# Decode attention with a gated MLP mixer: value products placed behind the second half of the scores, first keys loaded head by head, four tiny loads ahead of the output weights

## The chip, the cores and the metric

The kernel runs on one NeuronCore of a Trainium2 chip. The metric is the device time of one execution in microseconds (us), lower is better. A time "of the runs" is the median of several executions; a "span" is the stretch of one profiled execution that the profile covers, which is a little shorter than that execution's own time.

Five engines work side by side, each through its own list of instructions in order: TensorE (PE in the profile; its weight loads are PEld), VectorE (DVE), ScalarE (ACT), GpSimd (POOL) and SyncE (SP), which here issues the loads. Engines wait for one another through semaphores.

## The reference

One decode step for 8 batch rows. Attention over the last 1024 cached positions, with 16 query heads on 8 key/value heads of width 256, is mixed with an MLP of width 1792 through a sigmoid gate. Everything is bf16 with D = 448.

```python
W = min(4096, max(256, Sk // 4))                  # 1024 of 4096 positions
q = (x @ wq).reshape(B, Sq, Hq, Dh)               # Hq 16, Dh 256
scores = einsum("bhqd,bhkd->bhqk", q, k) * Dh ** -0.5
p = softmax(scores)
a = einsum("bhqk,bhkd->bhqd", p, v) ... @ wo
b = gelu(layernorm(x) @ w1 + b1) @ w2 + b2
g = sigmoid((x * gate_w).sum(-1))
out = g * a + (1 - g) * b
```

Keys and values of the window are 8 x 8 x 1024 x 256 x 2 bytes = 33.6 MB each; with the weights some 77.7 MB are read once.

## The kernel before, in words

**Units.** The cache is worked through in 16 units `u`: one batch row and 4 of the 8 key/value heads (`QUAD`). The keys of a unit are one tile of 128 partitions x 8192 bf16 (2 MB): partition 4s + a holds positions of head a, 32 consecutive ones (`kv_loader`, L109). The values of a unit have the same form.

**Loads.** All large loads go through `plan`, a list in a fixed order: keys 0, query weights, the MLP's weights, then keys u followed by values u-2 (`LAG` is 2), at the end values 14 and 15 and the output weights `wo` (L155 to L176). They share a ring of 9 slots of 2 MB. `pump` (L99) issues the next load on SyncE's queue as soon as `done` has been told that a slot's reader is recorded; in the built program a load's issue waits for that reader, and also for the landing of the load eight places ahead of it in the list, because eight completion semaphores take turns. The slot of the keys is released by the second `turn_keys` of the unit, that of the values by `values`.

**One turn of the loop** (L613 to L630) carries four units at different stages. The steps, by name:

- `turn_keys(u, hf)`, L356: VectorE turns half of the keys into `kt` (32x32 transposes).
- `scores(u, hf)`, L422 and L428: TensorE writes half of the scores into PSUM tile `S`: one product that masks foreign heads (L422) and eight with the keys (L428).
- `top(u-1)`, L440 and L442: VectorE takes the maximum `mx` of the previous unit's scores and spreads it into `m4`. `share(u-1)`, L448: a small fp32 product `mz` joins the maxima.
- `expo(u-1)`, L454 and L457: VectorE reduces `mz` to `nmx`; ScalarE computes `E = exp(S + nmx)` and its row sums.
- `turn(u-2)`, L470: VectorE transposes `E` into `ET`. `total(u-2)`, L481: TensorE adds up the row sums (`den`, fp32). `invert(u-2)`, L491 and L492: VectorE's reciprocal `rb`, ScalarE's `rsel`.
- `values(u-2)`, L500 and L509: sixteen TensorE products `PO <- slot, ET`, then ScalarE's copy `first` of one half of `PO`.
- `gather(u-3)`, L515: VectorE adds the other half of `PO` to `first`, giving `os_`. `finish(u-3)`, L530 and L533: fp32 products `fin`, copied by ScalarE into `oT`.

The order is written out by hand: the pool context is `manual_schedule`, so each engine executes its own steps in the order in which the Python calls them. In the loop `values(u-2)` stands between the two halves of `scores(u)` on TensorE, and `first(u-2)` and `rsel(u-2)` stand ahead of `E(u-1)` on ScalarE. `PO` is a single PSUM tile, the score tiles `S` are two, and the fp32 products `den`, `mz` and `fin` share two small tiles.

**After the loop** (L631 to L686) the last units run out: `turn`, `total`, `top(15)`, `share(15)`, `gather(13)`, `finish(13)`, `invert(14)`, `expo(15)`, `values(14)`, `turn(15)`, `total(15)`, `invert(15)`, `gather(14)`, `finish(14)`, then `spread_rows` (L655), `values(15)`, `gather(15)`, `finish(15)`, `spread_rows`, and `project` (L671): 128 small products with the output weights into `A_ps`, the mix `res` (L688) and four stores.

Of the kernel before, what the change touches and what calls it, by code (L numbers as in the profile page):

```python
# [11 lines left out]
BF16 = mybir.dt.bfloat16  # L12
# [6 lines left out]
def kernel(  # L19
# [15 lines left out]
    nc = tc.nc  # L35
    P = nc.NUM_PARTITIONS

    NB, Sq, D = A_x.shape
    _, Hkv, Sk, Dh = A_k_cache.shape
# [19 lines left out]
    QUAD = 4  # L59
    RQ = QUAD * rep  # L60
    NQ = NB * Hkv // QUAD
    SK = P // QUAD
    NCK = W // SK
# [9 lines left out]
    LAG = 2  # L73
# [7 lines left out]
    xf = A_x.rearrange("b s d -> (b s) d")  # L81
# [3 lines left out]
    consts = ctx.enter_context(tc.tile_pool(name="consts", bufs=1))  # L85
# [19 lines left out]
    def done(n=1):  # L105
        consumed[0] += n
        pump()

    def kv_loader(src, u, parts):  # L109
        b, half = divmod(u, Hkv // QUAD)  # L110
        v = src[b, half * QUAD : (half + 1) * QUAD, kv_base:Sk, :].rearrange(
            "a (s c) d -> s a (c d)", c=NCK
        )

        def load(t):
            n = NCK * Dh // parts
            for i in range(parts):
                nc.sync.dma_start(  # L118
                    t[:, i * n : (i + 1) * n], v[:, :, i * n : (i + 1) * n]
                )  # L120

        return load

    def rows_loader(pieces):
        def load(t):
            o = 0
            for ap in pieces:
                n = 1
                for s in ap.shape[1:]:
                    n *= s  # L130
                dst = t[:, o : o + n]
                if len(ap.shape) == 3:
                    dst = dst.rearrange("p (a n) -> p a n", a=ap.shape[1])
                nc.sync.dma_start(dst, ap)
                o += n

        return load
# [3 lines left out]
    def add(key, loader):  # L141
        index[key] = len(plan)
        plan.append(loader)

    def add_kv(name, src, u, parts=1):
        add((name, u), kv_loader(src, u, parts))

    wq_m = A_wq[0:DM, :].rearrange("(p r) n -> p (r n)", r=NR)
    wq_t = A_wq[DM:D, :].rearrange("r (h n) -> (r h) n", h=2)
# [2 lines left out]
    w2_v = B_w2.rearrange("(p c) n -> p (c n)", c=NF)  # L152
    wo_v = A_wo.rearrange("(q p j) n -> p q (j n)", p=P, j=NJ8)

    add_kv("k", A_k_cache, 0, parts=2)  # L155
    add(("wq", 0), rows_loader([wq_m[:, 0 : 2 * HD]]))
    add(("wq", 1), rows_loader([wq_m[:, 2 * HD : 3 * HD], wq_t]))
    add(("w1",), rows_loader([w1_m, w1_t]))
    add(("w2",), rows_loader([w2_v]))
    for u in range(1, NQ):  # L160
# [5 lines left out]
    for q in range(0, NHQ, 2):  # L166
        add(
            ("wo", q),
            rows_loader(
                [  # L170
                    wo_v[:, q + i, j0 * D : j1 * D]
                    for i in range(2)
                    for j0, j1 in WO_PARTS[q + i]
                ]
            ),
        )  # L176

    def slot(*key):
        return slots[index[key]]
# [172 lines left out]
    def turn_keys(u, hf):  # L352
        kn = slot("k", u)
        kt = ktpool.tile([P, CH, NK, BLK, NPAR], BF16, tag="kt", name="kt")
        KT[u, hf] = kt
        nc.vector.transpose(  # L356
            kt[:].rearrange("p c k x r -> p (c k x r)").bitcast(WORD),
            kn[:, hf * CH * Dh : (hf + 1) * CH * Dh].bitcast(WORD),
        )
        if hf == NH - 1:  # L360
            done()
# [55 lines left out]
    def scores(u, hf):  # L417
        if hf == 0:
            S[u] = ps_s.tile([P, W], F32, tag="S", name="S")
        cols = slice(hf * CH * BLK, (hf + 1) * CH * BLK)  # L420
        kt = KT.pop((u, hf))
        nc.tensor.matmul(  # L422
            S[u][:, cols], lhsT=foreign[:], rhs=place[:], start=True, stop=False
        )
        for k in range(NK):
            for par in range(NPAR):
                j, m = k // (NK // NJ), k % (NK // NJ) * NPAR + par
                nc.tensor.matmul(  # L428
                    S[u][:, cols],
                    lhsT=qw[:, j, u, m * RQ : m * RQ + P],  # L430
                    rhs=kt[:, :, k, :, par],
                    start=False,
                    stop=(k == NK - 1 and par == NPAR - 1),
                )

    soft = {}
# [8 lines left out]
    def share(u):  # L445
        m4 = soft.pop(u)
        mz = ps_sm.tile([P, QUAD], F32, tag="sm", name="mz")
        nc.tensor.matmul(mz[:], lhsT=same[:], rhs=m4[:], start=True, stop=True)  # L448
        soft[u] = mz

    def expo(u):
        mz = soft.pop(u)
        nmx = epool.tile([P, 1], F32, tag="nmx", name="nmx")
        nc.vector.reduce_max(nmx[:], mz[:], axis=AXIS.X, negate=True)  # L454
        E = epool.tile([P, NCK // PAIR, BLK, PAIR], BF16, tag="E", name="E")
        rowsum = epool.tile([P, 1], F32, tag="rowsum", name="rowsum")
        nc.scalar.activation(  # L457
            E[:].rearrange("p c x i -> p c i x"),
            S.pop(u)[:].rearrange("p (c i x) -> p c i x", i=PAIR, x=BLK),
            ACT.Exp,  # L460
            bias=nmx[:],
            scale=1.0,
            accum_out=rowsum[:],
        )
        soft[u] = (E, rowsum)

    def turn(u):
        E, rowsum = soft.pop(u)
        ET = epool.tile([P, NCK // PAIR, BLK, PAIR], BF16, tag="ET", name="ET")
        nc.vector.transpose(  # L470
            ET[:].rearrange("p c r i -> p (c r i)").bitcast(WORD),
            E[:].rearrange("p c x i -> p (c x i)").bitcast(WORD),
        )
        soft[u] = (ET, rowsum)

    den = {}

    def total(u):
        ET, rowsum = soft.pop(u)
        den[u] = ps_sm.tile([P, 1], F32, tag="sm", name="den")  # L480
        nc.tensor.matmul(  # L481
            den[u][:], lhsT=rowden[:], rhs=rowsum[:], start=True, stop=True
        )
        soft[u] = ET

    rsel = {}

    def invert(u):
        rsel[u] = opool.tile([P, RQ], F32, tag="rsel", name="rsel")
        rb = epool.tile([P, 1], F32, tag="rb", name="rb")  # L490
        nc.vector.reciprocal(rb[:], den.pop(u)[:])  # L491
        nc.scalar.activation(rsel[u][:], sel2[:], ACT.Copy, scale=rb[:])  # L492

    def values(u):
        ET = soft.pop(u)
        vn = slot("v", u)
        NG = NCK // PAIR
        for c in range(NG):
            t = c % QUAD
            nc.tensor.matmul(  # L500
                PO[32 * t : 32 * t + PAIR * RQ],
                lhsT=ET[:, c, 0:RQ, :],
                rhs=vn[:, PAIR * c * Dh : PAIR * (c + 1) * Dh],
                start=(c < QUAD),
                stop=(c >= NG - QUAD),
            )
        done()
        first = epool.tile([P, Dh], F32, tag="first", name="first")
        nc.scalar.activation(first[:], PO[:, 0, :], ACT.Copy, scale=own[:, 0:1])  # L509
        soft[u] = first  # L510

    def gather(u):
        first = soft.pop(u)
        os_ = epool.tile([P, Dh], F32, tag="os", name="os_")
        nc.vector.scalar_tensor_tensor(  # L515
            os_[:],
            in0=PO[:, 1, :],
            scalar=own[:, 1:2],
            in1=first[:],
            op0=ALU.mult,  # L520
            op1=ALU.add,
        )
        soft[u] = os_

    def finish(u):
        b, half = divmod(u, Hkv // QUAD)
        os_, rs = soft.pop(u), rsel.pop(u)
        sm = ps_sm.tile([P, NJ, RQ], F32, tag="sm", name="fin")
        for j in range(NJ):
            nc.tensor.matmul(  # L530
                sm[:, j, :], lhsT=os_[:, j::NJ], rhs=rs[:], start=True, stop=True
            )
        nc.scalar.copy(  # L533
            oT[:, half * RQ : (half + 1) * RQ, :, b].rearrange("p h j -> p j h"), sm[:]
        )
# [75 lines left out]
        scores(0, hf)  # L611
    mlp_out(hs)
    for u in range(1, NQ):  # L613
        turn_keys(u, 0)
        scores(u, 0)
        if u >= LAG + 1:
            gather(u - LAG - 1)
        if u >= LAG:
            turn(u - LAG)
            total(u - LAG)  # L620
        if u >= LAG + 1:
            finish(u - LAG - 1)
        top(u - 1)
        share(u - 1)
        turn_keys(u, 1)
        if u >= LAG:
            values(u - LAG)
            invert(u - LAG)
        scores(u, 1)
        expo(u - 1)  # L630
    u = NQ - 1  # L631
    turn(u - 1)
    total(u - 1)
    top(u)
    share(u)
    gather(u - 2)
    finish(u - 2)
    invert(u - 1)
    expo(u)
    values(u - 1)  # L640
    turn(u)
    total(u)
    invert(u)
    gather(u - 1)
    A_ps = ps_misc.tile([P, DO], F32, tag="misc", name="A_ps")
    nc.vector.memset(A_ps[:], 0.0)
    finish(u - 1)
# [81 lines left out]
```

## Time and profile before

| | |
|---|---|
| median of 3 runs | 194.02 us (192.89 to 194.35) |
| the profiled execution's own time | 192.88 us |
| its span | 191.1 us |
| TensorE busy | 135.0 us (71%) |
| VectorE busy | 128.0 us (67%) |
| ScalarE busy | 43.1 us (23%) |
| read from HBM | 77.68 MB, 407 GB/s over the span |
| granted TensorE clock, mean | 0.857 of full |

In a timeline line the first number is the start in us from the span's start, the second the duration, then engine, line, operation, what is written and read with shapes, the count of merged instructions, and in brackets the engine's idle time ahead of it and who ended it. In a line of windows the first columns are the stretch and its length, then the busy time and count of PE, PEld, DVE, ACT and POOL, then the granted TensorE clock (1.00 is full), the busy share of the DMA engines and GB/s. The chain that ended last is followed back from the last instruction to whatever released each step.

### The profile page before, as it was taken

How to read it: one execution, taken by the hardware profiler on the slowest of the kernel's cores; microseconds unless marked ns; L12 is line 12 of the kernel's file. 1: busy time of each engine (PE TensorE's matmuls, PEld its weight loads, DVE VectorE, ACT ScalarE, POOL GpSimd, SP SyncE). 2: the span in 40 equal slices, each digit the busy share in tenths (PEclk: the TensorE clock that was granted, in tenths of full speed). 3: DMA queues.
4: the chain of work that ended last, by engine and by line, in shares of the span. 5: the costliest groups of instructions: out<-in, count | busy, mean ns of one | idle time of the engine just before them, and what ended most of it. 6: DMA issues, size and time to landing. Idle time of an engine off the chain costs nothing.

```text
span 191.1 us, 2508 instructions
## 1 busy us (share of the span) xinstructions
PE 135.0 (71%) x1022; PEld 69.5 (36%) x1022; DVE 128.0 (67%) x186; ACT 43.1 (23%) x91; POOL 5.0 (3%) x7
## 2 busy tenths in 40 slices
PE   0035999794878489857666699859684999396773
PEld 0021864341424143424242254315331534144452
DVE  7876465995949494949493949494949585865310
ACT  2032220313040304040404013403140034042310
POOL 8100000000000000000000000000000000000000
PEclk9999657999699966999999558979998599997558
DMA  5999999999999999999999999999999999999980
GB/s 193 411 425 429 423 434 430 418 429 425 432 432 425 418 429 432 436 422 425 425 425 434 425 429 429 425 432 422 429 425 432 432 422 429 422 436 419 407 320 7
DMA packets 6734, 77.85 MB, mean 407 GB/s; under 512 B 945, under 2 KB 1346, under 8 KB 1986
## 3 DMA queue, kind: packets, MB, share of 16 engines
q1 hardware_dynamic: 6512, 77.67, 96.1%
q8 instruction: 8, 0.13, 0.3%
q10 hardware_dynamic: 210, 0.02, 0.1%
q14 instruction: 4, 0.03, 0.1%
HBM read 77.68 MB, written 0.01 MB: 407 GB/s over the span
## 4 chain that ended last, share of the span: by engine, by line
DMA 84%; PE 7%; DVE 3%; ACT 3%; SPq 1%; issue 1%
DMA slot<-in_A_k_cache_dram 77%; DMA slot<-in_A_wq_dram 7%; PE fin L530 2%; PE A_ps L671 2%; ACT E L457 1%; PE PO L500 1%; DVE kt L356 1%; PE S L428 1%; DVE ET L470 1%; SPq L118 1%; DVE mx L440 1%; ACT first L509 0%; PE mz L448 0%; ACT oT L533 0%; PE pp L655 0%
## 5 line engine op out<-in xcount | busy, mean ns | idle before, releaser
L356 DVE STREAM_TRANSPOSE kt<-slot 128x2048 int32<-128x2048 int32 x32 | 73.7, 2305 | 35.8 <-DMA slot<-in_A_k_cache_dram 35.8
L428 PE MATMUL S<-kt,qw 128*128 128x512 bf16 x256 | 71.0, 424 | 29.9 <-DVE kt L356 27.6
L428 PEld LDWEIGHTS <-qw 128*128 128x128 bf16 x256 | 26.7, 104 | 69.8 <-issue 48.9
L457 ACT ACTIVATE E<-S,nmx 128x1024 bf16<-128x1024 f32 x16 | 22.2, 1390 | 3.0 <-DVE nmx L454 3.0
L533 ACT CAST oT<-fin 128x16 bf16<-128x16 f32 x16 | 3.6, 227 | 82.2 <-PE fin L530 82.2
L500 PE MATMUL PO<-slot,ET 128*16 128x512 bf16 x256 | 20.9, 456 | 0.0
L440 DVE TENSOR_REDUCE mx<-S 128x1 f32<-128x1024 f32 x16 | 19.0, 1185 | 0.0
L509 ACT ACTIVATE first<-PO,own 128x256 f32<-128x256 f32 x16 | 7.6, 473 | 28.6 <-PE PO L500 28.5
L470 DVE STREAM_TRANSPOSE ET<-E 128x512 int32<-128x512 int32 x16 | 11.2, 697 | 4.2 <-ACT E L457 4.2
L422 PE MATMUL S<-place,foreign 128*128 128x512 bf16 x32 | 13.4, 418 | 0.1
L448 PE MATMUL mz<-m,same 128*128 128x4 f32 x32 | 6.8, 283 | 5.9 <-ACT oT L533 4.1
L481 PEld LDWEIGHTS den<-rowsum,rowden 128*128 128x128 f32 x32 | 7.2, 231 | 4.5 <-issue 1.4
L448 PEld LDWEIGHTS mz<-m,same 128*128 128x128 f32 x32 | 5.6, 215 | 7.3 <-ACT oT L533 5.3
L500 PEld LDWEIGHTS <-ET 128*16 128x16 bf16 x256 | 5.6, 96 | 5.5 <-issue 2.7
L422 PEld LDWEIGHTS <-foreign 128*128 128x128 bf16 x32 | 3.2, 101 | 9.4 <-issue 7.6
L481 PE MATMUL den<-rowsum,rowden 128*128 128x1 f32 x32 | 5.2, 233 | 0.0
L492 ACT ACTIVATE rsel<-sel,rb 128x8 f32<-128x8 f32 x16 | 4.7, 296 | 0.7 <-DVE rb L491 0.7
L413 DVE CAST qw<-qp 32x512 bf16<-32x512 f32 x4 | 2.7, 687 | 3.2 <-ACT qw L411 3.2
L370 PE MATMUL Sq<-slot,xT 128*8 128x512 bf16 x32 | 3.5, 558 | 1.7 <-DMA slot<-in_A_wq_dram 1.7
L291 POOL MEMSET qw<- 128x5120 bf16 x1 | 4.4, 4364 | 0.0
L442 DVE TENSOR_SCALAR m<-block,mx 128x4 f32<-128x4 f32 x16 | 3.7, 229 | 0.6
L454 DVE TENSOR_REDUCE nmx<-mz 128x1 f32<-128x4 f32 x16 | 2.3, 144 | 2.2 <-PE mz L448 2.1
(135 smaller groups left out, 84.7 us busy)
## 6 DMA issues: line engine op xcount, KB each, us to landing
slot<-in_A_v_cache_dram SPq DMA_DIRECT2D x16, 2048.0 KB, 36.8
slot<-in_A_k_cache_dram SPq DMA_DIRECT2D x15, 2048.0 KB, 39.1
slot<-in_A_wo_dram SPq DMA_DIRECT2D x3, 896.0 KB, 31.0
slot<-in_A_k_cache_dram SPq DMA_DIRECT2D x2, 1024.0 KB, 7.2
slot<-in_A_wq_dram SPq DMA_DIRECT2D x1, 2048.0 KB, 11.5
slot<-in_B_w_dram SPq DMA_DIRECT2D x1, 1568.0 KB
slot<-in_B_w_dram SPq DMA_DIRECT2D x1, 1344.0 KB
slot<-in_A_wq_dram SPq DMA_DIRECT2D x1, 1024.0 KB, 13.3
```

The lines of the kernel that those rows point to most:

```text
L291: nc.gpsimd.memset(qw[:], 0.0)
L356: nc.vector.transpose(kt[:].rearrange("p c k x r -> p (c k x r)").bitcast(WORD), kn[:, hf * CH * Dh : (hf + 1) * CH * Dh].bitcast(WORD),)
L422: nc.tensor.matmul(S[u][:, cols], lhsT=foreign[:], rhs=place[:], start=True, stop=False)
L428: nc.tensor.matmul(S[u][:, cols], lhsT=qw[:, j, u, m * RQ : m * RQ + P], rhs=kt[:, :, k, :, par], start=False, stop=(k == NK - 1 and par = ...
L440: nc.vector.reduce_max(mx[:], S[u][:], axis=AXIS.X)
L448: nc.tensor.matmul(mz[:], lhsT=same[:], rhs=m4[:], start=True, stop=True)
L457: nc.scalar.activation(E[:].rearrange("p c x i -> p c i x"), S.pop(u)[:].rearrange("p (c i x) -> p c i x", i=PAIR, x=BLK), ACT.Exp, bias=n ...
L470: nc.vector.transpose(ET[:].rearrange("p c r i -> p (c r i)").bitcast(WORD), E[:].rearrange("p c x i -> p (c x i)").bitcast(WORD),)
L481: nc.tensor.matmul(den[u][:], lhsT=rowden[:], rhs=rowsum[:], start=True, stop=True)
L492: nc.scalar.activation(rsel[u][:], sel2[:], ACT.Copy, scale=rb[:])
L500: nc.tensor.matmul(PO[32 * t : 32 * t + PAIR * RQ], lhsT=ET[:, c, 0:RQ, :], rhs=vn[:, PAIR * c * Dh : PAIR * (c + 1) * Dh], start=(c < QUA ...
L509: nc.scalar.activation(first[:], PO[:, 0, :], ACT.Copy, scale=own[:, 0:1])
```

## The change

Four things change. (1) In the loop `values(u-2)` moves behind the second half of the scores; `total(u-2)` moves to the front of the turn; `invert(u-2)` moves ahead of the second `turn_keys`; `finish(u-3)` directly follows `gather(u-3)`. (2) After the loop the same steps are put in another order: `values(14)` now stands ahead of `expo(15)`, and `total(14)` ahead of `turn(14)`. (3) The keys of unit 0 are loaded as four transfers, one per head, each into every fourth partition, in place of two transfers of half the columns. (4) Four tiny loads of 8, 4, 2 and 1 rows of 32 elements go on SyncE's queue ahead of the first output weights; nobody reads them.

```diff
@@ kv_loader, rows_loader, plan
-    def kv_loader(src, u, parts):
+    def kv_loader(src, u, by_head):
...
         def load(t):
-            n = NCK * Dh // parts
-            for i in range(parts):
-                nc.sync.dma_start(
-                    t[:, i * n : (i + 1) * n], v[:, :, i * n : (i + 1) * n]
-                )
+            if by_head:
+                for a in range(QUAD):
+                    nc.sync.dma_start(t[a::QUAD, :], v[:, a])
+            else:
+                nc.sync.dma_start(t[:], v)
...
-    def rows_loader(pieces):
+    def rows_loader(pieces, probes=()):
         def load(t):
             o = 0
+            for n in probes:
+                probe = consts.tile([NB, QUAD * RQ], BF16, name=f"probe{n}")
+                nc.sync.dma_start(probe[0:n, :], xf[0:n, 0 : QUAD * RQ])
             for ap in pieces:
...
-    add_kv("k", A_k_cache, 0, parts=2)
+    add_kv("k", A_k_cache, 0, by_head=True)
...
                     for j0, j1 in WO_PARTS[q + i]
-                ]
+                ],
+                probes=(8, 4, 2, 1) if q == 0 else (),
@@ the loop
     for u in range(1, NQ):
+        if u >= LAG:
+            total(u - LAG)
         turn_keys(u, 0)
         scores(u, 0)
         if u >= LAG + 1:
             gather(u - LAG - 1)
+            finish(u - LAG - 1)
         if u >= LAG:
             turn(u - LAG)
-            total(u - LAG)
-        if u >= LAG + 1:
-            finish(u - LAG - 1)
         top(u - 1)
         share(u - 1)
+        if u >= LAG:
+            invert(u - LAG)
         turn_keys(u, 1)
+        scores(u, 1)
         if u >= LAG:
             values(u - LAG)
-            invert(u - LAG)
-        scores(u, 1)
         expo(u - 1)
@@ after the loop
     u = NQ - 1
+    total(u - 1)
     turn(u - 1)
-    total(u - 1)
     top(u)
     share(u)
+    invert(u - 1)
     gather(u - 2)
+    values(u - 1)
+    expo(u)
     finish(u - 2)
-    invert(u - 1)
-    expo(u)
-    values(u - 1)
+    gather(u - 1)
+    total(u)
     turn(u)
-    total(u)
     invert(u)
-    gather(u - 1)
```

`turn` and `total` only pass the row sums along differently; what they compute is the same.

More of the change, by code (lines that the diff above doesn't have):

```diff
@@ L143, in add, with add_kv @@
         plan.append(loader)
-    def add_kv(name, src, u, parts=1):
-        add((name, u), kv_loader(src, u, parts))
+    def add_kv(name, src, u, by_head=False):
+        add((name, u), kv_loader(src, u, by_head))
     wq_m = A_wq[0:DM, :].rearrange("(p r) n -> p (r n)", r=NR)
@@ L467, in turn @@
     def turn(u):
-        E, rowsum = soft.pop(u)
+        E = soft.pop(u)
         ET = epool.tile([P, NCK // PAIR, BLK, PAIR], BF16, tag="ET", name="ET")
@@ L473, in turn @@
         )
-        soft[u] = (ET, rowsum)
+        soft[u] = ET
     den = {}
     def total(u):
-        ET, rowsum = soft.pop(u)
+        E, rowsum = soft.pop(u)
         den[u] = ps_sm.tile([P, 1], F32, tag="sm", name="den")
@@ L483, in total @@
         )
-        soft[u] = ET
+        soft[u] = E
     rsel = {}
```

## The prediction

> **What bounds the kernel now.** The page first:
>
> ```profile
> span 191.1 us, 2508 instructions
> ...
> DMA  5999999999999999999999999999999999999980
> ...
> DMA 84%; PE 7%; DVE 3%; ACT 3%; SPq 1%; issue 1%
> ```
>
> The loads run without a gap, and the chain follows them to 163.3 us, where the last keys land; from there it is computing. The next view is the timeline of one middle turn (keys landing at 94.5; the turns' first transposes start at 84.74, 94.54, 104.55, and eight turns to 163.31 give 9.82 us each):
>
> ```profile
> 94.54 2.31 DVE L356 STREAM_TRANSPOSE kt<-slot 128x2048 int32<-128x2048 int32 x1 [2.80 <-DMA slot<-in_A_k_cache_dram]
> 97.14 0.70 DVE L470 STREAM_TRANSPOSE ET<-E 128x512 int32<-128x512 int32 x1
> 97.76 1.19 DVE L440 TENSOR_REDUCE mx<-S 128x1 f32<-128x1024 f32 x1
> 98.98 0.23 DVE L442 TENSOR_SCALAR m<-block,mx 128x4 f32<-128x4 f32 x1
> 99.12 2.30 DVE L356 STREAM_TRANSPOSE kt<-slot 128x2048 int32<-128x2048 int32 x1
> 100.02 1.04 PE L500 MATMUL PO<-slot,ET 128*16 128x512 bf16 x16
> 101.11 0.47 ACT L509 ACTIVATE first<-PO,own 128x256 f32<-128x256 f32 x1 [1.46 <-PE PO L500]
> 101.47 1.90 PE L428 MATMUL S<-kt,qw 128*128 128x512 bf16 x8
> 101.72 1.38 ACT L457 ACTIVATE E<-S,nmx 128x1024 bf16<-128x1024 f32 x1
> ```
>
> The values are done while VectorE still turns the second keys, so `E` ends at 103.10, 4.05 us before its own transpose (107.15). VectorE waits 2.80 us for keys each turn: the loop has slack. The tail's timeline:
>
> ```profile
> 170.49 1.38 ACT L457 ACTIVATE E<-S,nmx 128x1024 bf16<-128x1024 f32 x1
> 171.95 0.71 DVE L470 STREAM_TRANSPOSE ET<-E 128x512 int32<-128x512 int32 x1 [1.64 <-ACT E L457]
> 172.58 1.19 DVE L440 TENSOR_REDUCE mx<-S 128x1 f32<-128x1024 f32 x1
> 175.88 1.43 ACT L457 ACTIVATE E<-S,nmx 128x1024 bf16<-128x1024 f32 x1
> 180.19 1.90 PE L500 MATMUL PO<-slot,ET 128*16 128x512 bf16 x15
> ```
>
> Here each step waits for the one before; the last loads end between 186.5 and 187 (33 GB/s in that half microsecond, none after), the last products at 187.9. So the tail's chain, about a microsecond longer than the loads, sets the end. Last, the windows, cut where the granted clock changes:
>
> ```profile
> 92.29:95.70 3.41, 1.50 (x7) 0.57 (x6) 1.16 (x1) 1.06 (x2) 0.00 (x0) 1.00 1.00 418
> ...
> 102.53:105.94 3.41, 1.06 (x5) 0.38 (x4) 1.39 (x1) 0.61 (x2) 0.00 (x0) 1.00 1.00 425
> 105.94:109.35 3.41, 2.44 (x6) 0.83 (x6) 3.37 (x6) 0.00 (x0) 0.00 (x0) 0.50 1.01 428
> ...
> 126.42:129.83 3.41, 3.34 (x8) 1.30 (x8) 3.37 (x6) 0.00 (x0) 0.00 (x0) 0.50 1.00 428
> ```
>
> A window with 1.06 us of TensorE work is followed by one at half clock; one with 1.50 is not; one with 1.36 us of large products and 0.3 of small ones (170.79 to 174.20) is; one with 3.34, all large products, ends the slow stretch (129.83 on is full).
>
> **What the Trainium skill says.** "TensorE: Matmul & The Clock Gate", section "What's actually happening": the clock is halved after an idle window of about 3.4 us and restored after a busy one, on windows that run freely. The trace agrees: stretches are multiples of 3.41 us, and the eight products of L428 take 1.90 us at full and 3.57 at half clock. Same page, "Architectural detail": ScalarE and VectorE are strictly first-in first-out, TensorE only pulls weight loads forward; so what stands behind `first` waits with it. No row contradicts this. "DMA: Bandwidth & Descriptors", "Why a DMA increments its semaphore by 16": a load runs on the largest number up to 16 that divides its slowest dimension; the four head loads (32 rows) would use 16 engines, the tiny ones 8, 4, 2, 1. No row here shows these shapes.
>
> **The loads, parts 3 and 4.** Keys 0: two issues (0.65 and 0.58 us) become four, each 0.3 to 0.65, so the query weights' issue slips from 2.06 to 3 us or so. Cover: keys 0 are 2 MB, 4.9 us at 425 GB/s, so the queue isn't empty. Both key halves now need all 2 MB: landing near 8.6 (1.44 plus the 7.2 us median); VectorE first wants them at 12.88, behind the normalization. Price 0; bounds -0.3 (earlier first bytes) to +1.5 (32 rows on every fourth partition move slower; the whole stream would follow). Tiny loads: four issues of 0.33 = 1.3 us of SyncE, and each takes a turn in the eight semaphores. By the built order the output weights' issues then wait four landings later: 143.7 to 168.2 becomes 163.3 to about 178.5, the last two behind the landing of tiny loads, which queue behind values 15 (landing near 178). The queue then still holds 3.5 MB, 8.2 us, ahead of the end; the last two pieces (0.45 MB) are needed only after 185. Price 0, bounds 0 to +0.3; without that cover some 2 us.
>
> Issues of keys and values: the key slot is released by the second `turn_keys` (issue at 101.45), landing 37 us later; the value slot is released 3.3 us later than now. With over 30 us queued, neither starves the stream.
>
> **The loop, part 1: the ring that closes.** `values(u-2)` now waits for the second scores, `first` for the values, and `E(u-1)` stands behind `first`. Queued behind `values` on TensorE is `total(u-1)`, which waits for `E(u-1)`, and behind it both the next scores. From one E's end to the next, at full clock, by VectorE: to its transpose 0.08 (171.87 to 171.95), to `mx` 0.62, to `m4` 1.22, to the second keys 0.14 plus 0.06 for the moved reciprocal (estimate from 101.35 and 101.40), keys 2.30, scores begin 0.05 later, eight products until the next can begin 1.74 (101.47 to 103.21, the next L422), values 1.04, `first` 0.05 later, E behind it 0.40 (101.11 to 101.51, the next start), E 1.38. Sum 9.08, against 9.82 of loads: slack falls from 4.05 to 0.74. By TensorE: `den` ends 0.48 after E (172.35), L422 0.22, first scores 1.90, `fin` 0.61, its copy 0.32, `mz` 0.39, L422 0.22, scores 1.74, values 1.04, then 1.83 as above: 8.75.
>
> Now the clock. From the values' end to the next first scores lie 0.05 + 0.40 + 1.38 + 0.48 = 2.3 us with only the tiny `den`. A window that covers 2.05 us or more of it holds at most those 1.36 us of large products; 2.3 us leave such positions (3.41 - 2.05) + (2.3 - 2.05) = 1.6 of 3.41 us, about half. Then the first scores run slow: up to 3.57 + 0.43 in place of 1.90 + 0.22, but one window of 3.41 costs at most 1.7. They fill that window, so the clock returns, and the TensorE ring is 8.75 + 1.7 = 10.4 at most. Three windows are 10.24: a turn near that length finds the next window at the same place, so the state holds itself. I take 10.2 a turn, +0.4 over the loads, for 11 turns: 4.4; entering it costs one slow half, 1.7 (the slack of 0.74 is by then used in the 0.4). **Lateness at the last keys: 6.1 us**, an estimate. Before, such windows cost nothing, since E hung on no scores.
>
> **The tail, part 2**, first without lateness. Second keys 167.95 to 170.25; scores to 172.04, values(13) to 173.08, `first` 173.13, E(14) 173.53 to 174.91: 3.04 later than 171.87. Transpose 174.99, `mx` 175.61, `m4` 176.83, `mz` (0.29 and 0.51) to 177.63. Then values(14) comes ahead of E(15), at half clock as now: 1.88, to 179.5; `first`, E(15) at 180.0, 4.1 later than 175.88. `den` of 15 ends 2.1 after that start as now (182.1), `fin` 1.0, copy and spread 0.48: values(15) at 183.6 instead of 180.19. From there all is as before: **+3.4**. At full clock values(14) and `fin` would give back 1.2: +2.2.
>
> **Sum.** Against the profiled execution (192.88, span 191.1): 192.9 + 6.1 + 3.4 = 202.4. This execution is the fastest shown; the median stands 1.1 above it, and I add half of that: **203**.
>
> **Rivals.** (a) *The loop keeps pace.* For: 9.08 is under 9.82, and where a window falls differs between executions. Then only the tail counts: 192.9 + 3.4 = 196.3. (b) *Slow windows last.* A first half that begins late in its window doesn't fill it; then second scores and values run slow too: the VectorE ring becomes 9.08 + 1.67 + 0.84 = 11.6. For: 68.39 to 75.22 took two windows. Half of 11 turns at +1.8 instead of +0.4 add 7.7; with fewer such turns (a third) 5: about 208. (c) *Hidden.* If E(14) came no later, nothing but order changes: 193 to 194. Against: its chain has no branch around `values`. (d) *Faster: the stream levels out.* If lateness doesn't arise and the smaller pieces even out the DMA engines, the fade after 184 (0.54 MB, 1.26 us at full rate, taking 2.8) ends 1.5 sooner, first bytes 0.5 sooner, and the last products, now 0.7 behind, follow: 190.2. It decides only where the tail's chain is shorter than the loads, against the +3.4. That the moves happen as written follows from the hand-written order.
>
> **Numbers.** Forecast 0.52 (own range 199.5 to 206), (a) 0.27, (b) 0.12, (c) 0.06, (d) 0.03. Leaving out (b), (c), (d) except their near edges, the range is 195.5 to 207, with the clock-full tail (-1.2) and the loads' +1.5 inside. One per cent is about what a measurement tells: faster 0.03, same 0.05, slower 0.92.
>
> **What would show it.** E(u-1) starting 0.4 after `first(u-2)` in every turn; the idle of L356 on keys (35.8 us) nearly gone and turns 10.0 to 10.3 apart; half-clock windows under the first scores in most turns; the last keys' transpose near 169 though the load lands at 163; E(15) behind `first(14)`, 5.1 us after E(14) ends; DMA slices empty from about 187. If turns stay 9.8 apart and L356 still waits, (a) holds. The forecast is wrong if the clock's threshold lies lower than 1.06 to 1.5 us, or if the loads' stream itself changes.

## The result and the profile after

The changed kernel takes 203.89 us in the median of four executions (200.68 to 206.48); the kernel before, run beside it, takes 193.58 us (192.89 to 194.35). The ratio is 1.041, its 95% interval 1.030 to 1.052. It is less than the quotient of the two medians, 1.053, because every ratio here leaves out executions in a slower state, among them the two longest of the changed kernel and, later, one of 241.91 us of the kernel before with added products, at a granted clock of 0.604. The profiled execution took 202.46 us, 9.6 more than that of before.

The page of the changed kernel (its lines stand three to five further down than in the kernel before: L360 is `turn_keys`, L485 `den`, L513 `first`), and below it two rows of the page of before:

```profile
span 200.6 us, 2517 instructions
...
PEclk9999999999997958796969696969576969696555
DMA  5999999999999999999999999999999999999100
...
PE 63%; ACT 13%; DVE 9%; DMA 8%; issue 4%; SPq 0%; ACTq 0%
...
L360 DVE STREAM_TRANSPOSE kt<-slot 128x2048 int32<-128x2048 int32 x32 | 73.5, 2300 | 13.1 <-DMA slot<-in_A_k_cache_dram 13.0
...
L485 PE MATMUL den<-rowsum,rowden 128*128 128x1 f32 x32 | 6.5, 273 | 28.7 <-ACT E L461 28.7
...
L513 ACT ACTIVATE first<-PO,own 128x256 f32<-128x256 f32 x16 | 7.6, 473 | 57.6 <-PE PO L504 57.6
```

```profile
PEclk9999657999699966999999558979998599997558
...
L356 DVE STREAM_TRANSPOSE kt<-slot 128x2048 int32<-128x2048 int32 x32 | 73.7, 2305 | 35.8 <-DMA slot<-in_A_k_cache_dram 35.8
```

The chain that ended last has gone from the loads (84%, now 8%) to TensorE (7%, now 63%). VectorE waits 13.1 us for keys in place of 35.8, and TensorE waits 28.7 us for `E` at `den`. The loads end at 187.3 us, as before to within a microsecond; the last thirteen microseconds of the span are computing alone. In the clock's row (`PEclk`, in tenths of full speed) a half-clock window now returns at an even pitch.

The timeline of one turn, from `E(13)` to `E(14)`:

```profile
169.75 1.38 ACT L461 ACTIVATE E<-S,nmx 128x1024 bf16<-128x1024 f32 x1
171.23 0.38 PE L485 MATMUL den<-rowsum,rowden 128*128 128x1 f32 x2 [1.96 <-ACT E L461]
171.47 0.38 PE L426 MATMUL S<-place,foreign 128*128 128x512 bf16 x1
171.69 3.47 PE L432 MATMUL S<-kt,qw 128*128 128x512 bf16 x8
173.28 2.29 DVE L360 STREAM_TRANSPOSE kt<-slot 128x2048 int32<-128x2048 int32 x1
174.95 0.67 PE L534 MATMUL fin<-rsel,os__1413 128*128 128x8 f32 x4
175.93 0.39 PE L452 MATMUL mz<-m,same 128*128 128x4 f32 x2 [0.32 <-ACT oT L537]
176.39 1.91 PE L432 MATMUL S<-kt,qw 128*128 128x512 bf16 x8
178.22 1.04 PE L504 MATMUL PO<-slot,ET 128*16 128x512 bf16 x16
179.38 0.47 ACT L513 ACTIVATE first<-PO,own 128x256 f32<-128x256 f32 x1 [3.35 <-PE PO L504]
179.75 1.38 ACT L461 ACTIVATE E<-S,nmx 128x1024 bf16<-128x1024 f32 x1
```

This is the ring: `E`, `den` behind it, both halves of the scores, the values, `first`, and 0.37 us after its start the next `E`, 10.00 us after the last. The first scores take 3.47 us and the second 1.91; nothing here waits for keys.

The windows from 161.58 on, cut where the clock changes:

```profile
161.58:164.99 3.41, 3.41 (x10) 1.29 (x8) 3.37 (x5) 0.00 (x0) 0.00 (x0) 0.50 0.98 418
164.99:168.41 3.42, 3.10 (x20) 1.63 (x23) 2.62 (x3) 0.37 (x2) 0.00 (x0) 1.00 1.02 436
168.41:171.82 3.41, 1.45 (x20) 0.64 (x13) 1.42 (x3) 1.79 (x3) 0.00 (x0) 1.00 0.99 423
171.82:175.23 3.41, 3.41 (x11) 1.51 (x9) 3.37 (x5) 0.00 (x0) 0.00 (x0) 0.50 1.00 428
175.23:178.65 3.42, 3.10 (x22) 1.51 (x26) 0.50 (x2) 0.37 (x2) 0.00 (x0) 1.00 0.97 408
178.65:182.06 3.41, 1.00 (x14) 0.40 (x6) 0.86 (x2) 1.79 (x3) 0.00 (x0) 1.00 1.01 417
182.06:185.48 3.42, 2.14 (x18) 0.90 (x18) 1.80 (x5) 0.30 (x1) 0.00 (x0) 0.50 0.97 386
```

Every third window is at half clock. It follows a window in which TensorE has only 1.00 or 1.45 us of work: the one that holds `first`, `E` and the wait for it.

The tail's timeline:

```profile
183.86 1.88 PE L504 MATMUL PO<-slot,ET 128*16 128x512 bf16 x16
185.85 0.47 ACT L513 ACTIVATE first<-PO,own 128x256 f32<-128x256 f32 x1 [2.15 <-PE PO L504]
186.22 1.38 ACT L461 ACTIVATE E<-S,nmx 128x1024 bf16<-128x1024 f32 x1
189.62 1.90 PE L504 MATMUL PO<-slot,ET 128*16 128x512 bf16 x15
197.39 0.33 DVE L693 SCALAR_TENSOR_TENSOR res<-A_ps,gg_s,mixb 128x112 bf16<-128x112 f32 x1 [2.66 <-PE A_ps L676]
```

`E(15)` starts 5.10 us after the end of `E(14)` (181.12), behind `values(14)` and `first(14)`. `res` comes at 197.39 in place of 187.89: 9.5 us later, the whole difference.

### The profile page after: what moved, and what is told of

The parts are those of the page before. It is cut to its first block, busy times and chain, and to the rows that moved or that the text cites. A ratio compares the mean times of both kernels' runs of the same rounds, so it can differ in the third digit from the quotient of the medians.

```text
span 200.6 us, 2517 instructions
## 1 busy us (share of the span) xinstructions
PE 142.6 (71%) x1022; PEld 71.1 (35%) x1022; DVE 130.8 (65%) x186; ACT 42.2 (21%) x91; POOL 5.0 (2%) x7
## 4 chain that ended last, share of the span: by engine, by line
PE 63%; ACT 13%; DVE 9%; DMA 8%; issue 4%; SPq 0%; ACTq 0%
PE S L432 35%; ACT E L461 11%; PE PO L504 9%; DMA slot<-in_A_wq_dram 7%; DVE kt L360 4%; PE fin L534 4%; PE S L426 4%; PE mz L452 3%; PE den L485 3%; DVE mx L444 2%; DMA slot<-in_A_k_cache_dram 2%; ACT oT L537 2%; PE A_ps L676 2%; PE hT L557 1%; PE hT L547 1%
## 5 line engine op out<-in xcount | busy, mean ns | idle before, releaser
L432 PE MATMUL S<-kt,qw 128*128 128x512 bf16 x256 | 82.1, 476 | 3.3 <-DVE nmx L458 3.3
L360 DVE STREAM_TRANSPOSE kt<-slot 128x2048 int32<-128x2048 int32 x32 | 73.5, 2300 | 13.1 <-DMA slot<-in_A_k_cache_dram 13.0
L432 PEld LDWEIGHTS <-qw 128*128 128x128 bf16 x256 | 29.1, 114 | 44.6 <-issue 28.2
L485 PE MATMUL den<-rowsum,rowden 128*128 128x1 f32 x32 | 6.5, 273 | 28.7 <-ACT E L461 28.7
L513 ACT ACTIVATE first<-PO,own 128x256 f32<-128x256 f32 x16 | 7.6, 473 | 57.6 <-PE PO L504 57.6
L504 PE MATMUL PO<-slot,ET 128*16 128x512 bf16 x256 | 18.4, 410 | 0.0
L485 PEld LDWEIGHTS den<-rowsum,rowden 128*128 128x128 f32 x32 | 5.3, 206 | 35.9 <-ACT E L461 35.8
L426 PEld LDWEIGHTS <-foreign 128*128 128x128 bf16 x32 | 6.0, 189 | 0.4 <-issue 0.3
```

Source lines behind the costliest of these rows:

```text
L360: nc.vector.transpose(kt[:].rearrange("p c k x r -> p (c k x r)").bitcast(WORD), kn[:, hf * CH * Dh : (hf + 1) * CH * Dh].bitcast(WORD),)
L426: nc.tensor.matmul(S[u][:, cols], lhsT=foreign[:], rhs=place[:], start=True, stop=False)
L432: nc.tensor.matmul(S[u][:, cols], lhsT=qw[:, j, u, m * RQ : m * RQ + P], rhs=kt[:, :, k, :, par], start=False, stop=(k == NK - 1 and par = ...
L485: nc.tensor.matmul(den[u][:], lhsT=rowden[:], rhs=rowsum[:], start=True, stop=True)
L504: nc.tensor.matmul(PO[32 * t : 32 * t + PAIR * RQ], lhsT=ET[:, c, 0:RQ, :], rhs=vn[:, PAIR * c * Dh : PAIR * (c + 1) * Dh], start=(c < QUA ...
```

## The experiments

**One part at a time.** Four kernels split the change: the loads alone, the new order with the old loads, the loop's order alone, the tail's order alone.

```diff
@@ loads alone: the kernel before, and
-    add_kv("k", A_k_cache, 0, parts=2)
+    add_kv("k", A_k_cache, 0, by_head=True)
...
+                probes=(8, 4, 2, 1) if q == 0 else (),
@@ order alone: the changed kernel, and
-    add_kv("k", A_k_cache, 0, by_head=True)
+    add_kv("k", A_k_cache, 0, parts=2)
...
-                probes=(8, 4, 2, 1) if q == 0 else (),
@@ loop alone: order alone, the calls after the loop as before
@@ tail alone: the kernel before, the calls after the loop as in the changed one
```

> The kernel before with the two load changes alone: first keys as four head loads, four tiny loads ahead of the output weights; all steps in the old order. Theory (the order is the cause): the last keys land 0 to 1 us later (after the change they landed at 164.3 instead of 163.3 in the traces), so 193.5 to 194.6 us, and exponentials still end about 4 us ahead of their transposes. Rival (the loads cause the loss): 200 us or more.

> The changed kernel with the old loads: the new order in the loop and behind it alone. Theory: nearly the whole loss, 201 to 205 us, turns of about 10.2 us and half clock under the first scores in most turns. Rival (the loads cause the loss): 193 to 195 us.

> The new order in the loop, the old order behind the loop, old loads. Theory: the exponential of unit 14 comes 9 us later than before (3.0 by order, 6 by late turns), and only the 0.3 to 0.4 us of the tail's own order are saved: 201 to 204 us. Rival (the order behind the loop is a large part): 197 us or less.

> The old order in the loop, the new order behind it, old loads. Theory: the exponential of unit 15 waits for the values of unit 14 and starts about 1 us later, of which 0.4 us reach the values of unit 15: 193.6 to 194.6 us. Rival (the tail's order costs the 3.4 us): 197 us.

| | median us | ratio to before, interval | turn, E(3) to E(14) | E(14) starts |
|---|---|---|---|---|
| before (median of the runs beside the four parts) | 193.81 | 1 | 9.81 | 170.49 |
| loads alone | 194.08 | 1.0032 (0.9995 to 1.0068) | 9.69 | 171.69 |
| order alone | 203.76 | 1.044 (1.032 to 1.055) | 10.25 | 182.35 |
| loop alone | 202.92 | 1.047 (1.038 to 1.057) | 10.13 | 179.82 |
| tail alone | 193.54 | 0.998 (0.995 to 1.001) | 9.65 | 170.46 |
| changed kernel | 203.89 | 1.041 (1.030 to 1.052) | 10.27 | 179.75 |

In the old order of the loop `E` comes unevenly (turns of 7 to 13 us), so the three means below 9.9 say no more than that the loop keeps pace. The trace of order alone is of its longest execution (204.98 us), which has four turns of 11.1 to 11.7 us where that of the changed kernel has two of 11.4.

The loop's order accounts for the whole loss. The tail's order by itself costs nothing that these runs can tell; the loads cost 0.3%, with an interval that just reaches nothing. In their profile the transfer rate in the second slice of the span is 322 GB/s in place of 411, the first keys that VectorE waits for are turned at 31.93 in place of 30.97, and `res` comes at 188.50 in place of 187.89. The five traces with the new first loads have 322 to 393 GB/s in that slice and the seven with the old ones 411 to 433, long before the tiny loads are issued at 145 us. So a delay well inside the allowed bound of +1.5 shows in these traces, and its beginning belongs to the head loads. With the new order it adds nothing that can be told: order alone and the changed kernel take the same. The two load changes were not run apart to the end. The issues of the output weights come about as predicted, from 164.38 to 180.4 us in the changed kernel where 163.3 to 178.5 were given, and no product waits for them there.

**What closes the ring.** If `E(u-1)` is late because it stands behind `first(u-2)`, calling it ahead of the values must give everything back, with the values still behind the second scores.

```diff
@@ the changed kernel, the loop
         scores(u, 1)
+        expo(u - 1)
         if u >= LAG:
             values(u - LAG)
-        expo(u - 1)
```

> The changed kernel with two calls of the loop exchanged: the exponential of unit u-1 ahead of the values of unit u-2, so on ScalarE it no longer stands behind the copy first(u-2); the values stay behind the second scores. Theory (the loss comes from the exponential that hangs on the values): E starts about 0.2 us after the second keys are turned, as before; only the small order effect of the tail remains: 193.5 to 195.5 us. Rival (the values' place behind the scores itself, or the loads, cost the time): 200 us or more.

193.73 us, ratio 1.001 (0.998 to 1.004), turns of 9.74, VectorE's wait for keys back at 34.8 us. All of the loss hangs on that one place in ScalarE's order.

Is the values' place enough, or must `total(u-2)` stand at the front of the turn as well?

```diff
@@ the kernel before, the loop
+        scores(u, 1)
         if u >= LAG:
             values(u - LAG)
             invert(u - LAG)
-        scores(u, 1)
         expo(u - 1)
```

> The kernel before with one edit: in the loop values(u-2) and the invert(u-2) behind it are called after scores(u, 1). total, finish, the tail and the loads stay as they were. Theory (the place of the values alone closes the ring: E(u-1) stands behind first(u-2), and the next first scores wait for E(u-1) through the two score tiles even without den ahead of them; the stretch from the values' end to the next first scores holds some 1.9 us without large products, 0.05 + 0.40 + 1.38, in place of 2.3): turns of 9.9 to 10.3 us, half-clock windows under the first scores in most turns, E(14) starting at 177 to 180 in place of 170.5, and 199 to 204 us. Rival (total at the front of the turn is what closes the ring, the values' place is harmless): turns of 9.8, E(14) at 170 to 173, and 193 to 196 us.

203.66 us, ratio 1.055 (1.048 to 1.062), turns of 10.12, `E(14)` at 181.03. The values' place is enough. Its timeline shows how the ring closes without `den` ahead of the scores:

```profile
129.44 0.47 ACT L509 ACTIVATE first<-PO,own 128x256 f32<-128x256 f32 x1 [3.44 <-PE PO L500]
...
130.00 1.37 ACT L457 ACTIVATE E<-S,nmx 128x1024 bf16<-128x1024 f32 x1
...
131.47 0.38 PE L422 MATMUL S<-place,foreign 128*128 128x512 bf16 x1 [2.09 <-ACT E L457]
131.69 3.13 PE L428 MATMUL S<-kt,qw 128*128 128x512 bf16 x8
```

The masking product L422 itself waits 2.09 us for `E`: there are two score tiles, and `E(u-1)` has to read one before the scores of u+1 can overwrite it. In the changed kernel `den` waits for the same `E` in the same place, so it hides this second wait. That it adds little is seen from the turns: 10.12 us here, 10.13 with the whole order of the loop.

The other way round, `total` was put back where it had been, in an otherwise unchanged copy of the changed kernel:

```diff
@@ the changed kernel, the loop
-        if u >= LAG:
-            total(u - LAG)
         turn_keys(u, 0)
...
             turn(u - LAG)
+            total(u - LAG)
         top(u - 1)
```

> The changed kernel with total(u-2) put back behind the first scores, where it was. Theory: the first scores no longer wait for the exponential through the row sums at the head of TensorE's list; with late turns they follow the values at once, the idle stretch that slows the clock is gone, and turns keep near the loads' pace: 196 to 199 us. Rival (VectorE's ring, through the exponential's transpose, sets the turn): no change, 202 to 205 us.

242.16 us, ratio 1.251 (1.237 to 1.264), turns of 13.6. Neither theory had this. The timeline of one turn:

```profile
99.72 0.38 PE L426 MATMUL S<-place,foreign 128*128 128x512 bf16 x1 [1.96 <-ACT E L461]
99.94 2.99 PE L432 MATMUL S<-kt,qw 128*128 128x512 bf16 x8
...
103.43 0.56 PE L485 MATMUL den<-rowsum,rowden 128*128 128x1 f32 x2
...
104.04 0.17 DVE L495 RECIPROCAL rb<-den 128x1 f32<-128x1 f32 x1 [2.25 <-PE den L485]
104.12 2.29 DVE L360 STREAM_TRANSPOSE kt<-slot 128x2048 int32<-128x2048 int32 x1
...
106.47 3.57 PE L432 MATMUL S<-kt,qw 128*128 128x512 bf16 x8 [1.53 <-DVE nmx L458]
```

`invert(u-2)` stayed ahead of the second `turn_keys`. Its reciprocal waits 2.25 us for `den`, which now stands behind the first scores and `fin`; the second keys are queued behind the reciprocal. First scores and second keys, which the changed kernel works on side by side (171.69 and 173.28 in its turn above), lie one behind the other, and both halves of the scores are slower than at full clock. So with `invert` ahead of the second keys, `total` belongs ahead of the first scores. The expectation had looked at TensorE's order alone.

**The clock.** If half-clock windows make the ring longer than the loads, the ring with *more* TensorE work must be faster. Twelve products of 512 columns, which nobody reads (called fillers below), go into two places of the changed kernel's turn; as a control, six go into one place of the kernel before.

```diff
+    def fill(n):
...
+        for _ in range(n):
+            nc.tensor.matmul(
+                warm[0][:], lhsT=foreign[:], rhs=place[:], start=True, stop=True
+            )
@@ the changed kernel, the loop: fill(6) ahead of scores(u, 1) and behind values(u - LAG)
@@ the kernel before, the loop: fill(6) behind scores(u, 1)
```

> The changed kernel plus twelve extra 512-column products per turn into a scratch PSUM tile that nothing reads: six (1.3 us at full clock) behind the values, where TensorE waits for the exponential, and six ahead of the second scores, where it waits for the keys. Theory (half-clock windows lengthen the turn): no window is idle enough, the clock stays full in the loop, turns follow the loads at 9.8 us and only the 3.0 + 0.4 us of the order remain: 196 to 198.5 us, though with more work in it. Rival (the ring is longer than the loads' pace at any clock): 202 us or more, since the extra work can only delay.

> The kernel before plus six extra 512-column products per turn behind the second scores (scratch, read by nothing). Theory: half-clock windows cost the old order nothing, since its exponential hangs on no later product: 193 to 194.5 us, with half-clock windows fewer in the loop. Rival (the clock is worth microseconds in either order): 191.5 us or less.

The filled changed kernel takes 196.66 us (196.5 to 196.81), ratio 1.017 (1.008 to 1.025), where the unfilled one stands at 1.041, though the filled one has 1.46 us more of work at either place. Its mean granted clock is 0.963 in place of 0.835. The two ratios are 2.4% apart, some 4.8 us. The page and one ring of it:

```profile
PEclk9999999999999999999999999999999999999555
```

```profile
165.20 1.39 ACT L461 ACTIVATE E<-S,nmx 128x1024 bf16<-128x1024 f32 x1
...
166.69 0.38 PE L485 MATMUL den<-rowsum,rowden 128*128 128x1 f32 x2 [0.57 <-ACT E L461]
...
167.15 1.91 PE L432 MATMUL S<-kt,qw 128*128 128x512 bf16 x8
...
174.85 1.38 ACT L461 ACTIVATE E<-S,nmx 128x1024 bf16<-128x1024 f32 x1
```

The first scores take 1.91 us and the turn 9.65. That is a little less than the loads take, 9.79 us from one unit's keys to the next: VectorE's wait for keys grows from 1.22 us at 56.31 to 2.52 at 163.95, so this ring catches up with the loads. The four executions of the unfilled kernel point the same way: 200.68 us at a mean clock of 0.851, 202.46 at 0.835, 205.32 at 0.819 and 206.48 at 0.811. The control stays at 193.01, ratio 0.998 (0.995 to 1.001): with the old order, slow windows in the loop cost nothing that can be told.

**A version a little faster than both.** In the tail of the kernel before, the half clock lies in the chain. The control got further products there: six behind `total(14)`, two behind `total(15)`, four behind `values(15)`.

```diff
@@ the kernel before with fill(6) in the loop, and after the loop
     total(u - 1)
+    fill(6)
...
     total(u)
+    fill(2)
...
     values(u)
+    warm[0] = ps_s.tile([P, QN], F32, tag="S", name="warm2")
+    fill(4)
```

> The kernel before, with six products of 512 columns in each turn of the loop as in the earlier run with such products, and in the tail six behind total(14), two behind total(15) and four behind values(15); nobody reads them. Theory (the tail's half clock is in its chain: values(15) takes 1.90 us in place of 1.04, and the last 128 products run at half clock): the tail is shorter by 0.9 to 1.7 us of chain, but the last output weights land at 186.7, which leaves about 0.9 of it: 192.0 to 193.0 us, the ratio 0.990 to 0.997. Rival (the loads set the end, or the added products stand in the chain for as much as they give back): 193.0 to 194.5 us, ratio 0.997 to 1.005.

192.49 us (192.13 to 192.78) beside 193.59, ratio 0.9945 (0.9907 to 0.9983): half a per cent. Whether this is faster than the control too, the two intervals don't tell. Its chain and the end of its timeline:

```profile
DMA 93%; DVE 4%; SPq 1%; issue 0%; PE 0%
```

```profile
179.94 1.05 PE L500 MATMUL PO<-slot,ET 128*16 128x512 bf16 x15
...
184.97 0.57 PE L684 MATMUL A_ps<-slot,oP 128*8 128x112 bf16 x32 [0.79 <-DMA slot<-in_A_wo_dram]
...
187.17 0.27 PE L684 MATMUL A_ps<-slot,oP 128*8 128x112 bf16 x8 [0.29 <-DMA slot<-in_A_wo_dram]
187.50 0.33 DVE L703 SCALAR_TENSOR_TENSOR res<-A_ps,gg_s,mixb 128x112 bf16<-128x112 f32 x1 [3.76 <-PE A_ps L684]
```

The values take 1.05 us in place of 1.90, and now the last products wait for the output weights: the tail's chain has dropped under the loads, which leave no more than the 0.4 us that `res` has gained here.

## Why the prediction was right, step by step

Forecast 203, measured 203.89; the sum of 202.4 was made against the profiled execution of before, and that of the changed kernel took 202.46. The mechanism was right, but that the sum fits to 0.1 us is luck in part: its terms were off by up to 0.7 us, in both directions. Against the 193.58 us of the kernel before, the forecast is a ratio of 1.049, in the upper part of the measured interval.

**The ring.** Right. `E` starts 0.37 after `first` in the turn shown, as the 0.40 of the prediction has it, and the run with `E` called first shows that this place is the cause. The prediction named `den` as what hands the delay to the next scores; the score tiles do it as well, so that link was one of two.

**Its length.** The sum was right, its parts only roughly. At full clock the ring keeps pace with the loads: with fillers, turns of 9.67 between `E(3)` and `E(14)`. (Six of the fillers stand in that ring, at 169.99 to 171.28 us, so the 9.08 of the prediction was not measured itself.) At the clock as it is, nine of the eleven turns take 9.87 to 10.32, 10.02 in the mean, in place of the 10.2 taken, and two take 11.4: those where two half-clock windows stand together, at 69.4 and 141.1. That is rival (b)'s turn (predicted at 11.6) in two places of eleven. Together 113.0 us against 107.9, 5.1 more where 4.4 were predicted; `E(14)` is 9.26 later than before, and less the 3.04 of the order in its own turn and these 5.1, 1.1 is left for the entry where 1.7 was taken. Lateness 6.2, predicted 6.1: the two errors, +0.7 and -0.6, nearly cancel. The split between entry and turns is less sure than its sum, since `E` of before comes unevenly in the third turn.

**The side that is longer.** Wrong in a detail. VectorE's side was the longer one at full clock (9.08 to 8.75). In the slow turn it is TensorE's: from `E` to `E` 1.48 to `den`, 0.24 and 0.22 to the scores, 3.26 until `fin`, 0.70 and 0.28 until `mz`, 0.24 and 0.22, 1.83 of scores, 1.16 of values and 0.37, in all 10.00, under the 10.4 given as its most. The second keys are ready at 175.57, 0.82 before the second scores start. So the last keys' transposes were not all late by 6: the second came at 173.28 (5.4 later), the first at 166.44 (3.1 later, where 169 was given), for it waits for no `E`. And L360's wait for keys fell to 13.1, not to nearly nothing; 7.6 of that lies between 60 and 180 us, where it was 28.8.

**The tail.** Right: `E(15)` starts 5.10 after the end of `E(14)`, as given. Of its +3.4, 3.04 belong to the loop's order, which the last turn too has to pass. The remaining 0.4 was the tail's own order. The traces have less: from the start of `E(14)` to `values(15)` pass 9.87 us in the changed kernel and 9.70 in the kernel before, both with `values(14)` at half clock, so 0.2. The times of the runs can't tell it from nothing.

**The rivals.** (a), the loop keeps pace, was given 196.3: that is the filled kernel, measured at 196.66. That the figures are so close is luck in part. `E(14)` starts at 174.85 there, 1.3 later than the 173.53 of the prediction, and `values(14)` at full clock gives 0.9 back: from `E(14)` to `E(15)` pass 5.56 us where 6.47 were counted. What decides between (a) and the forecast is the clock. By the two ratios the order costs 1.7% at most, the fillers' own delay among it, and the half-clock windows 2.4% more. (c) and (d) needed an `E(14)` that isn't late. The loads, priced at nothing, cost 0.3% alone, within their bounds.

**The threshold.** It held where the forecast needed it: windows with 1.00 and 1.45 us of TensorE work, small products among it, were followed by half clock. The Trainium skill ("TensorE: Matmul & The Clock Gate", section "HAM oscillation — how this bites in real kernels") has as its rule that TensorE shouldn't idle for more than about 3.4 us at a time. Here the clock was halved with no idle stretch longer than 1.96 us in the two windows shown, and in the kernel before a stretch of 3.11 us (until 96.90), which lies across two windows, left it full. What tells the cases apart in these traces is how much 512-column work a window holds. At full clock, from 42 us on, the changed kernel's windows with 1.40 us of it or less are followed by half clock, and those with 1.56 or more are not.

**One or two half-clock windows.** The same measure, taken of the half-clock windows, tells which turns take 10.0 and which 11.4 us. In these lines the first busy time is that of the score products alone, the next two are of VectorE and ScalarE reading the scores:

```profile
69.43:72.85 3.42, 2.13 (x6) 0.88 (x1) 0.00 (x0) 0.50 1.00 426
130.87:134.29 3.42, 2.69 (x7) 0.88 (x1) 0.00 (x0) 0.50 1.00 426
141.11:144.53 3.42, 2.00 (x6) 0.51 (x1) 0.00 (x0) 0.50 1.02 436
```

The two with 2.13 and 2.00 us are followed by a second half-clock window; of the nine other stretches that begin between 69 and 175 us none is, and 2.69 is the least that they hold. TensorE's busy time as a whole is a poorer measure: it is 3.10 us in the window at 69.43 and 3.34 in the one at 130.87. The part that it lacks is the stretch of `fin`, the wait for its copy and `mz` (71.36 to 73.12). That fits the reason that rival (b) gave: a slow first half that doesn't fill its window. With all 512-column products counted, from 27 to 180 us, the half-clock windows of all twelve traces divide between 2.58 and 2.60 us, and those at full clock between 1.46 and 1.52, where the two groups overlap a little; the prediction worked with a line between 1.36 and 1.50. What stays open is the cause behind these lines: no run was made to move one window across.

## What to carry to other kernels

Before a step is moved on one engine, follow it through the queue of every engine that it releases: here sixteen products moved by one place put `E` behind `first` on ScalarE and turned a loop with 4 us of slack into a ring that at its own clock is longer than the loads. Add up such a ring at the clock that its own gaps will get, not at the clock of the trace before. Where it then is too long, try calling the step that the ring waits for (`E`) ahead of the one that can wait (`values` and `first`): here that gave the whole loss back. Products that nobody reads can be cheaper than a gap.

## What the runs showed that was not expected

- More TensorE work made the kernel faster: twelve products a turn, about 2.9 us of it, brought the ratio to the kernel before from 1.041 to 1.017.
- The ring locks to the clock's windows. From 69.4 to 171.8 us a half-clock stretch begins every 10.24 us, three windows of 3.41, in all eleven turns. Most turns take about 10.0, so the scores slide ahead of the window by some 0.2 us a turn, until too little of them is left in it (2.69 us at 130.87, then 2.00 at 141.11). The second half-clock window that follows makes that turn 11.4 long and brings the scores back. The mean turn is 10.27.
- One small product (0.38 us), put behind the first scores in TensorE's queue, cost some 40 us over the kernel (ratios 1.251 and 1.041), because a reciprocal of 0.17 us ahead of a 2.29 us transpose waited for it.
